# Moving one VectorE pass over the second weight ahead of the turns of batch 1's query features

## The chip, the cores and the metric

The kernel runs on one core of a Trainium2 chip. The metric is the device time of one execution in microseconds (us); before the change the median of three runs is 103.25 us. Engines are named as in the profile: PE is TensorE (matmuls), DVE is VectorE, ACT is ScalarE, POOL is GpSimd, SP is SyncE, which here only issues DMAs.

## What is computed

A linear attention with sketched features, and behind it a block with a hidden layer and a residual:

```python
# q, k, v: (4, 4, 1088, 32) f32; S1, S2: (8, 32)
def phi(x):
    a = np.einsum('rd,bhsd->bhsr', S1, x)
    b = np.einsum('rd,bhsd->bhsr', S2, x)
    return np.einsum('bhsi,bhsj->bhsij', a, b).reshape(*x.shape[:-1], r * r)
q_p, k_p = (phi(q), phi(k))
kv = np.einsum('bhsf,bhsd->bhfd', k_p, v)
z = np.sum(k_p, axis=2)
num = np.einsum('bhsf,bhfd->bhsd', q_p, kv)
den = np.einsum('bhsf,bhf->bhs', q_p, z)[..., None] + 1e-06
x = (num / den)      # heads side by side: (4, 1088, 128)
...
xn = (x - mu) / np.sqrt(var + 1e-06) * g_ln
ch = np.maximum(xn @ w_ch1, 0.0) @ w_ch2      # (128, 512), (512, 128)
return (x + ch).astype(np.float32)
```

The sketches and the two weights come as 64-bit floats. The chip's engines compute in 32 bits here, so the kernel builds 32-bit floats out of the two words of each number.

## The kernel before

All steps of the four batches are small functions ("ops"), and one long string, `PROGRAM` (line 910), lists their calls in the order in which they are issued. An op's instructions go to the engine that its function or its first argument names (V is VectorE, A ScalarE, G GpSimd, S SyncE's DMA queue), and each engine works through its own instructions in the order of the list. Between engines only data and buffers make one wait for another. So a call's place in the list matters against the other calls of its own engine.

The second weight (`w2` in the code, words numbered 2) goes through these passes, all on 128 x 512 words:

- `w_bits` (line 281): VectorE cuts the fraction bits out of each high word, one `tensor_scalar` with a bitwise and.
- `w_mant` (line 294): ScalarE makes the mantissa of them.
- `w_ex` (line 276): VectorE cuts the exponent out of the high words; ScalarE's `w_exf` and `w_e2` work on it, and VectorE's `w_e3` joins it with the sign.
- `w_add` and `w_mul`: GpSimd adds the low word's part to the mantissa, and multiplies.

Around the change, batch 0's rows enter the hidden layer, batch 1's query features are made, and batch 2's keys are begun. There are eight PSUM banks, A, B, C, D, M, N, O and K. The ops in question:

- `turn_g k 2` and `turn_r k 2` (lines 432 and 448): VectorE transposes the key rows of batch 2 into `kT`.
- `q_feat 1` (line 625): TensorE makes batch 1's query features, head h into bank A, B, C or D.
- `q_tok 1 h` (line 637): VectorE turns head h's features out of its bank into `fq`, here called the turn of bank B, A, D or C (heads 1, 0, 3, 2 in this order). It sets the bank free.
- `hid z c j` (line 841): TensorE multiplies batch 0's rows with block j of the first weight into bank z; `relu` (line 847) takes it out on ScalarE. The order of the banks is O, N, M, K, B, D, C; the last three need a turn to be over.
- `q_turn 4 9` (line 676): VectorE transposes a part of batch 0's query products, `qp`.
- `k_feat 2` (line 503): TensorE makes batch 2's key features in banks A and B, and `k_tok 2` (line 515) turns them on VectorE.
- `k_prod G 1 0 5`, `sk_qq 3` and `k_prod G 1 5 9` (lines 521 and 424): GpSimd forms the key products of batch 1 in two parts, with a small copy between them. All of its operands lie in SBUF.
- `k_val 1` (line 558): TensorE multiplies these products with batch 1's values, in bank K.

SyncE's queue holds, at the same place in the list, the loads of keys and queries of batches 2 and 3 (`ld`, line 111) and of the values.

Of the kernel before, what the change touches and what calls it, by code (L numbers as in the profile page):

```python
# [24 lines left out]
def kernel(  # L25
# [21 lines left out]
    B, H, S, D = q.shape  # L47
# [4 lines left out]
    G = S // 32  # L52
# [15 lines left out]
    M, KV = [banks["M"]], banks["K"]  # L68
# [863 lines left out]
    q_flip 2 4 0 C; ld_v S 1 2; q_flcp A 2 4 1 A; k_zs 1; f_spr B; q_flip 0 2 0 O; turn_h q 1 1;  # L932
    q_flcp A 2 4 0 C; ld_v S 1 1; f_rcp A B; q_flip 0 2 1 D; q_flcp A 0 2 0 O; k_sc 1;
    turn_h q 1 0; ld_vr S 1 1; num0 2 4 N; q_flcp A 0 2 1 D; k_sccp V 1; num0 0 2 O; turn_r k 2;
    k_prod G 1 0 5; num0_cp A 2 4 N; turn_g k 2 0 4; kv_rd S 0; q_feat 1 0 9; num0_cp A 0 2 O;
    ld_v S 1 0; hid O 0 0 0 2; q_tok 1 1 0 9; ld_vr S 2 0; hid N 0 2 2 4; q_tok 1 0 0 9;
    relu A O 0 0 0 2; ld S k 3 0 34; hid M 0 2 0 2; w_bits V 2 0 512; sk_qq 3; ld S q 2 0 34;
    hid K 0 3 0 2; k_prod G 1 5 9; q_tok 1 3 0 9; ld S q 3 0 34; hid B 0 1 2 4; q_tok 1 2 0 9;
    hid D 0 0 2 4; q_turn 4 9; relu A B 0 1 2 4; hid C 0 1 0 2; w_mant A 2 0 512; k_feat 2 0 9;
    relu A K 0 3 0 2; q_ac G 1 4 9; relu A C 0 1 0 2; relu A M 0 2 0 2; q_ac G 1 0 4; k_val 1;  # L940
# [96 lines left out]
```

## Time and profile before

| what | before |
| --- | --- |
| time, median of 3 runs (lowest to highest) | 103.25 us (103.06 to 103.25) |
| the profiled execution: time | 103.13 us |
| the profiled execution: span of the core | 101.3 us |
| granted TensorE clock, mean | 1.0 |
| TensorE busy | 95.2 us, 94% |
| VectorE busy | 71.5 us, 71% |
| ScalarE busy | 40.6 us, 40% |
| GpSimd busy | 60.5 us, 60% |

The span is the time from the first to the last instruction of the profiled execution; its time is longer by what lies before and behind. Busy shares are means over the whole span. A timeline row gives the start in us from the start of the span, the duration, the engine, the line, the operation, and "out<-in" with partitions x elements; in square brackets stands how long the engine sat idle before it, and what ended that. A line like L82 is that of a helper that several ops use. The starts of instructions that follow each other on an engine often lie a little before the end of the one in front.

### The profile page before, as it was taken

What the parts mean: (1) busy time and instruction counts of PE and PEld (TensorE: products, weight loads), DVE (VectorE), ACT (ScalarE), POOL (GpSimd) and SP (SyncE); (2) the same over time, 40 slices, a digit from 0 to 9 for tenths busy, and PEclk for the clock granted to TensorE, in tenths of its full rate; (3) what the DMA queues carried; (4) which work ended last, traced back from release to release, by engine and by line L of the source; (5) the groups of instructions that cost most, each with busy time, mean ns of one, the idle gap of its engine ahead of it and who ended that gap; (6) DMA issues with size and microseconds to landing.
All of it is one profiled execution on the core that took longest, in us unless ns stands there. A gap on an engine that the chain in (4) does not pass through costs nothing.

```text
span 101.3 us, 3442 instructions
## 1 busy us (share of the span) xinstructions
PE 95.2 (94%) x1348; PEld 68.8 (68%) x1348; DVE 71.5 (71%) x234; ACT 40.6 (40%) x118; POOL 60.5 (60%) x84
## 2 busy tenths in 40 slices
PE   5989999997999999999999999999999999999970
PEld 4856865855574597874686896864388985489950
DVE  1598999779998896989517889567239848483540
ACT  4465517653764900054482405456861004040300
POOL 7137979997377999300299997999529230004700
PEclk9999999999999999999999999999999999999999
DMA  2899991047954166623052720257244744630441
GB/s 86 283 315 399 354 323 44 10 128 193 380 204 123 56 193 206 181 60 129 6 179 73 177 46 6 83 173 209 85 117 102 223 151 134 183 108 0 104 109 46
DMA packets 14863, 15.16 MB, mean 150 GB/s; under 512 B 4096, under 2 KB 11136, under 8 KB 14848
## 3 DMA queue, kind: packets, MB, share of 16 engines
q1 hardware_dynamic: 13680, 13.61, 43.0%
q10 hardware_dynamic: 1168, 1.35, 5.3%
q8 instruction: 10, 0.16, 0.6%
q14 instruction: 5, 0.04, 0.1%
HBM read 10.42 MB, written 4.52 MB: 148 GB/s over the span
## 4 chain that ended last, share of the span: by engine, by line
PE 85%; DVE 6%; DMA 2%; ACT 1%; issue 1%; SPq 0%; DVEq 0%
PE bankO L859 8%; PE bankK L859 6%; PE bankN L859 6%; PE bankM L859 5%; PE bankD L843 5%; PE bankA L843 5%; PE bankK L561 5%; PE bankN L843 4%; PE bankM L250 4%; PE bankB L843 4%; PE bankM L843 4%; PE bankC L843 3%; PE bankA L735 3%; PE bankA L507 3%; PE bankC L859 3%; PE bankO L843 3%
## 5 line engine op out<-in xcount | busy, mean ns | idle before, releaser
L827 POOL TENSOR_SCALAR va<-mv 128x4 f32<-128x4 f32 (+1 forms) x10 | 2.3, 227 | 24.4 <-DVE mv L822 15.5
L82 POOL TENSOR_TENSOR kp<-kf 128x1280 f32<-128x1280 f32 (+4 forms) x9 | 15.7, 1749 | 1.9 <-PE bankK L561 1.8
L82 POOL TENSOR_TENSOR qp<-a,fq 128x1280 f32<-128x1280 f32 (+1 forms) x7 | 15.4, 2205 | 0.3
L677 DVE STREAM_TRANSPOSE qpT<-qp 128x1280 f32<-128x1280 f32 (+1 forms) x7 | 9.7, 1385 | 3.8 <-POOL qp L82 3.7
L250 PE MATMUL bankM<-ones 128*128 128x256 f32 (+1 forms) x34 | 9.3, 415 | 1.2 <-DVE top L180 1.2
L829 POOL TENSOR_TENSOR rstd<-va,mhalf 128x4 f32<-128x4 f32 (+1 forms) x10 | 9.4, 943 | 0.8
L859 PEld LDWEIGHTS bankO<-w,hT 128*128 128x128 f32 x64 | 7.6, 192 | 1.4 <-issue 0.9
L250 PEld LDWEIGHTS bankM<-ones 128*128 128x128 f32 x34 | 6.8, 223 | 2.6 <-DVE top L180 1.2
L859 PE MATMUL bankO<-w,hT 128*128 128x128 f32 x64 | 8.4, 280 | 0.0
L859 PEld LDWEIGHTS bankN<-w,hT 128*128 128x128 f32 x56 | 6.9, 192 | 1.4 <-issue 1.0
L859 PEld LDWEIGHTS bankK<-w,hT 128*128 128x128 f32 x56 | 6.9, 192 | 1.4 <-issue 1.4
L859 PE MATMUL bankK<-w,hT 128*128 128x128 f32 x56 | 7.3, 277 | 0.0
L816 DVE BATCH_NORM_STATS2 st<-x 128x6 f32<-128x128 f32 x32 | 6.8, 276 | 0.5 <-DMA x<-xd 0.5
L859 PE MATMUL bankN<-w,hT 128*128 128x128 f32 x56 | 7.1, 275 | 0.0
L797 DVE STREAM_TRANSPOSE xh<-xT 128x512 f32<-128x512 f32 x8 | 5.5, 690 | 2.1 <-ACT xT L77 2.0
L843 PE MATMUL bankD<-xT,w 128*128 128x512 f32 (+1 forms) x12 | 5.8, 566 | 0.8 <-DVE fq L639 0.8
L851 ACT ACTIVATE hT<-bankD 128x512 f32<-128x512 f32 (+1 forms) x6 | 3.4, 564 | 7.8 <-DMA x<-xd 7.3
L859 PEld LDWEIGHTS bankM<-w,hT 128*128 128x128 f32 x48 | 5.8, 192 | 0.9 <-issue 0.9
L859 PE MATMUL bankM<-w,hT 128*128 128x128 f32 x48 | 6.1, 277 | 0.0
L735 PE MATMUL bankD<-qpT,kvr 32*32 32x288 f32 (+1 forms) x64 | 5.9, 386 | 0.0
L735 PE MATMUL bankC<-qpT,kvr 32*32 32x288 f32 (+1 forms) x64 | 5.9, 386 | 0.0
L735 PE MATMUL bankB<-qpT,kvr 32*32 32x288 f32 (+1 forms) x64 | 5.8, 386 | 0.0
(227 smaller groups left out, 249.3 us busy)
## 6 DMA issues: line engine op xcount, KB each, us to landing
xd<-xh SPq DMA_DIRECT2D x8, 256.0 KB, 2.0
x<-xd SPq DMA_DIRECT2D x32, 64.0 KB, 2.0
kn<-in_k_dram SPq DMA_DIRECT2D x3, 544.0 KB
qn<-in_q_dram SPq DMA_DIRECT2D x3, 544.0 KB, 7.0
vn<-in_v_dram SPq DMA_DIRECT2D x12, 128.0 KB, 2.6
out_dram<-ob ACTq DMA_DIRECT2D x19, 64.0 KB, 1.9
out_dram<-ob SPq DMA_DIRECT2D x13, 64.0 KB, 3.6
w_raw<-in_moe_w_ch_dram SPq DMA_DIRECT2D x2, 256.0 KB, 5.0
```

Source lines behind the costliest of these rows:

```text
L82: by[eng].tensor_tensor(out=o, in0=a, in1=b, op=ALU.mult)
L250: pe.matmul(M[0][:, 0:w], ones[:, 0:P], ones[:, 0:w], start=True, stop=True)
L507: pe.matmul(X[hp][32 * g : 32 * g + 32, 32 * u0 : 32 * u0 + w], sk8[64 * hp : 64 * hp + 64, :], _ap(kT[b % 2], 64 * hp, 64, 32 * g + P * u ...
L561: pe.matmul(KV[D * h : D * h + D, 0:F], vn[b][:, TW * h + D * u : TW * h + D * (u + 1)], kp[:, H * F * u + F * h : H * F * u + F * (h + 1) ...
L677: dve.transpose(_ap(qpT, 0, P, 32 * u0, [[32, u1 - u0], [TW, 8], [1, 32]]), qp[:, H * F * u0 : H * F * u1])
L735: pe.matmul(X[r][D * h : D * h + D, o : o + w], kvr[b % 2][rows, F * h + D * f : F * h + D * f + D], qpT[rows, c : c + w], start=(f == 0), ...
L797: dve.transpose(_ap(xh[slot(c)], 0, P, 0, [[32, n], [32 * n, 4], [1, 32]]), cols(c))
L816: dve.bn_stats(out=sts[slot(c)][:, 6 * t : 6 * t + 6], in_=row_ap(c, t))
L829: pool.tensor_tensor(out=rstds[slot(c)][:, 0:n], in0=vas[slot(c)][:, 0:n], in1=mhalf[:, 0:n], op=ALU.pow)
L843: pe.matmul(banks[z][:, 0:n], w1[:, P * j : P * (j + 1)], cols(c)[:, a : a + n], start=True, stop=True)
L851: act.activation(o, i, AF.Relu)
L859: pe.matmul(banks[z][:, DM * t : DM * (t + 1)], h[:, 512 * j + P * t : 512 * j + P * (t + 1)], w2[:, DM * j : DM * (j + 1)], start=(j == 0 ...
```

## The change

The call `w_bits V 2 0 512` moves up in the list, from behind `hid M 0 2 0 2` to behind `turn_g k 2 0 4`. In VectorE's own order it stood between the turns of banks A and D, and now stands ahead of all four, behind the key transposes of batch 2. The calls that it passes in the list and that aren't VectorE's keep their order on their engines.

```diff
-    k_prod G 1 0 5; num0_cp A 2 4 N; turn_g k 2 0 4; kv_rd S 0; q_feat 1 0 9; num0_cp A 0 2 O;
-    ld_v S 1 0; hid O 0 0 0 2; q_tok 1 1 0 9; ld_vr S 2 0; hid N 0 2 2 4; q_tok 1 0 0 9;
-    relu A O 0 0 0 2; ld S k 3 0 34; hid M 0 2 0 2; w_bits V 2 0 512; sk_qq 3; ld S q 2 0 34;
+    k_prod G 1 0 5; num0_cp A 2 4 N; turn_g k 2 0 4; w_bits V 2 0 512; kv_rd S 0; q_feat 1 0 9;
+    num0_cp A 0 2 O; ld_v S 1 0; hid O 0 0 0 2; q_tok 1 1 0 9; ld_vr S 2 0; hid N 0 2 2 4;
+    q_tok 1 0 0 9; relu A O 0 0 0 2; ld S k 3 0 34; hid M 0 2 0 2; sk_qq 3; ld S q 2 0 34;
     hid K 0 3 0 2; k_prod G 1 5 9; q_tok 1 3 0 9; ld S q 3 0 34; hid B 0 1 2 4; q_tok 1 2 0 9;
```

## The prediction, made before the change was run

> **What bounds the kernel now.** I read the page first, then the waits of TensorE, then the chain of work that ended last, and last the timelines of the four engines around the edit.
>
> ```profile
> span 101.3 us, 3442 instructions
> ```
>
> ```profile
> PE bankM L250 <- DVE top L180: 1.2, 1, 1.2
> PE bankD L843 <- DVE fq L639: 0.8, 1, 0.8
> PE bankA L507 <- DVE kT L452: 0.5, 1, 0.5
> PE bankK L561 <- ACT vn L77: 0.2, 1, 0.2
> ```
>
> These four rows are all that TensorE ever waits for (columns: total us, times, longest). Apart from the first, which is the start of the program, the largest is one wait of 0.8 us: a hidden-layer matmul into bank D, held up by VectorE's turn of batch 1's query features (fq, line 639). A span that is TensorE work from end to end gets shorter only where such a wait goes. The chain shows what is in front of this one:
>
> ```profile
> 23.43 1.66 DVE bits L282
> 25.09 0.40 DVE fq L639
> ```
>
> The chain leaves TensorE for the first pass over the second weight's words, `w_bits` (line 282), 1.66 us of it, and comes back through the turn of head 3. So the moved instruction itself is on the path. VectorE's timeline around it (start, duration):
>
> ```profile
> 20.77 1.21 DVE L434 STREAM_TRANSPOSE kT<-kn 128x1024 f32<-128x1024 f32 x1
> 22.59 0.48 DVE L639 STREAM_TRANSPOSE fq<-bankB 128x288 f32<-128x288 f32 x1 [0.61 <-PE bankD L629]
> 22.99 0.44 DVE L639 STREAM_TRANSPOSE fq<-bankA 128x288 f32<-128x288 f32 x1
> 23.36 1.73 DVE L282 TENSOR_SCALAR bits<-w_raw 128x512 uint32<-128x512 uint32 x1
> 25.01 0.47 DVE L639 STREAM_TRANSPOSE fq<-bankD 128x288 f32<-128x288 f32 x1
> 25.41 0.43 DVE L639 STREAM_TRANSPOSE fq<-bankC 128x288 f32<-128x288 f32 x1
> 25.77 1.46 DVE L677 STREAM_TRANSPOSE qpT<-qp 128x1280 f32<-128x1280 f32 x1
> 27.49 0.48 DVE L517 STREAM_TRANSPOSE kf<-bankB 128x288 f32<-128x288 f32 x1 [0.25 <-PE bankB L507]
> 28.26 0.39 DVE L277 TENSOR_SCALAR ex<-w_raw 128x512 uint32<-128x512 uint32 x1
> ```
>
> `w_bits` takes 1.73 us. The last row is the same kind of instruction, with the same shape and the same input (`w_ex`), and takes 0.39. So some 1.34 us of `w_bits` is a stall, and it isn't a semaphore, because the instruction counts as running. GpSimd's timeline shows what runs beside it:
>
> ```profile
> 20.39 2.38 POOL L82 TENSOR_TENSOR kp<-kf 128x1280 f32<-128x1280 f32 x1
> 22.71 0.19 POOL L425 COPY skq<-skq 128x16 f32<-128x16 f32 x1
> 22.86 1.94 POOL L82 TENSOR_TENSOR kp<-kf 128x1024 f32<-128x1024 f32 x1
> 25.93 0.94 POOL L82 TENSOR_TENSOR ac<-fq 128x160 f32<-128x160 f32 x2 [1.12 <-DVE fq L639]
> 28.62 1.95 POOL L82 TENSOR_TENSOR kp<-kf 128x1024 f32<-128x1024 f32 x1 [1.76 <-PE bankK L561]
> ```
>
> The product of the key features (third row) ends at 22.86 + 1.94 = 24.80, and `w_bits` ends at 23.36 + 1.73 = 25.09, 0.29 later, a little less than its own 0.39. It reads as if `w_bits` stood until GpSimd's instruction was over and then ran. `w_ex` had the same work and met no GpSimd instruction: nothing ran there until 28.62. An early place shows the same between the two engines, in the first fence VectorE, in the second GpSimd:
>
> ```profile
> 4.05 0.16 DVE L207 TENSOR_TENSOR m<-bit,head 128x4 f32<-128x4 int32 x1
> 5.01 0.44 DVE L207 TENSOR_TENSOR m<-bit,head 128x2 f32<-128x2 int32 x1
> ```
>
> ```profile
> 4.98 0.45 POOL L82 TENSOR_TENSOR s_f<-mant,bits 16x128 f32<-16x128 f32 x1 [2.27 <-DVE bit L206]
> ```
>
> The mask of half the size takes 0.44 instead of 0.16 us and ends (5.45) just behind the GpSimd product that began before it (5.43).
>
> The Trainium skill, "SBUF — State Buffer", section "Who interferes with whom", has a rule for this that speaks against the new place as well: VectorE and GpSimd share a pair of ports, a `tensor_scalar` may need it, and whoever begins first keeps it for a whole instruction while the other stands. The trace agrees at 24.80 and 5.43. By that rule `w_bits` stands at the new place too, behind the product that began at 20.39; were there no such rule, it would take 0.39 there, and the sum below would come out the same, as the turns it delays have time to spare.
>
> **The change part by part.** One VectorE instruction moves. It issues no DMA; what it passes on its own engine are the turns of banks B and A (heads 1 and 0). The loads, matmuls and activations between the two places in the listing are on other engines, whose own order stays. Nothing is added or removed.
>
> *Its new place.* The key transpose in front ends at 20.77 + 1.21 = 21.98; VectorE then sat idle for 0.61 us, until TensorE gave it the query features at 22.59. `w_bits` begins at about 21.9, in the middle of GpSimd's product of 20.39, which ends at 22.77. I take it that VectorE gets its turn there: it ends at 22.77 + 0.29 = 23.06. No row shows `w_bits` at a place like this. Bounds: 22.3, if nothing holds it up (21.9 + 0.39), and 25.09, if it also stands through the two GpSimd instructions behind (second and third row of that fence). I take 23.06, since both rows with a stall end just behind the GpSimd instruction that had begun before, and one row, if a weak one, has such a change of turns, VectorE first and GpSimd second:
>
> ```profile
> 14.62 0.25 DVE L355 TENSOR_SCALAR cg<-ident,g_raw 128x128 f32<-128x128 f32 x1
> ```
>
> ```profile
> 13.99 0.72 POOL L323 TENSOR_TENSOR mant<-mant,low 128x256 f32<-128x256 f32 x1
> 14.78 0.53 POOL L82 TENSOR_TENSOR ac<-fq 128x160 f32<-128x160 f32 x1
> ```
>
> This `tensor_scalar` began beside one GpSimd instruction (over at 14.71), ended at 14.87, and the next one, begun at 14.78, took 0.53 where the pair of 25.93 took 0.47 each. So VectorE got in between. But GpSimd had a gap of 0.07 there, while at 22.7 its rows overlap.
>
> *The turns.* With starts 0.40, 0.37 and 0.36 apart as in the rows: B at 23.0 (0.4 later than now), A at 23.4, D at 23.77 to 24.24, C at 24.13 to 24.56. D ends 1.24 earlier than now (25.48), C 1.28 earlier (25.84).
>
> *TensorE behind them.*
>
> ```profile
> 23.66 0.59 PE L843 MATMUL bankK<-xT,w 128*128 128x256 f32 x2
> 24.09 0.59 PE L843 MATMUL bankB<-xT,w 128*128 128x256 f32 x2
> 25.54 0.70 PE L843 MATMUL bankD<-xT,w 128*128 128x256 f32 x2 [0.85 <-DVE fq L639]
> 26.07 0.59 PE L843 MATMUL bankC<-xT,w 128*128 128x256 f32 x2
> 26.60 0.43 PE L507 MATMUL bankA<-kT,sk 64*32 64x288 f32 x1
> 27.24 1.21 PE L561 MATMUL bankK<-kp,vn 128*32 128x64 f32 x72
> ```
>
> Bank B is needed at 24.09 and is turned at 23.48: 0.6 to spare, so the 0.4 costs nothing. The matmuls before B follow each other every 0.43 (23.66 to 24.09). Bank D's then begins at 24.52 (its turn is over 0.28 before) and bank C's at 24.95 (0.39 before). C's was at 26.07: **1.12 us** go, 0.85 of them the wait and the rest the slow start behind it (0.70, and 0.53 to the next). Then the key features follow at 25.48 and the key-value product at 26.12.
>
> *What is late next.* ScalarE:
>
> ```profile
> 24.72 0.39 ACT L851 ACTIVATE hT<-bankB 128x256 f32<-128x256 f32 x1 [1.34 <-PE bankB L843]
> 25.12 0.72 ACT L296 ACTIVATE mant<-bits,one 128x512 f32<-128x512 uint32 x1
> 25.75 0.36 ACT L851 ACTIVATE hT<-bankK 128x256 f32<-128x256 f32 x1
> ```
>
> Key features need bank B emptied: 25.11, against 25.48. The key-value product needs bank K emptied: 26.11, or about 26.0, as `mant` no longer waits for the bits; against 26.12. That one is close and may take back up to 0.05. It also needs GpSimd's second product, which begins some 0.25 later and ends at about 25.1: in time. VectorE's long turn of qp runs from 24.5 to 25.95, before bank B's keys (25.48 + 0.89 = 26.37). `w_ex` then comes at about 27.1 and is over at 27.5, when GpSimd's next product begins (28.62 − 1.1): no new stall, but by some hundredths only.
>
> *Loads don't come earlier.* The key rows of batch 3 are the first such input behind the edit; the queue's row, then DMA by the microsecond (last two columns: share of the engines, GB/s):
>
> ```profile
> 23.10 0.43 SPq L113 DMA_DIRECT2D kn<-in_k_dram  x1
> ```
>
> ```profile
> 28.00:29.00 1.00, 1.00 (x76) 0.79 (x70) 1.00 (x4) 0.32 (x1) 0.38 (x1) 1.00 0.94 383
> 29.00:30.00 1.00, 1.00 (x51) 0.71 (x48) 0.85 (x5) 0.78 (x4) 1.00 (x1) 1.00 0.24 77
> ```
>
> They are the first of three large loads issued one after another, and all three are through at about 29.0, so the first, by its third of the bytes, lands at about 26.5; VectorE will want it at 28.7, as its part there follows the key features. From there on what the four engines do hangs on work that itself moves up, GpSimd's product of the second weight too:
>
> ```profile
> 32.49 1.28 POOL L82 TENSOR_TENSOR w<-mant,bits 128x512 f32<-128x512 f32 x1 [0.69 <-DVE bits L318]
> ```
>
> It waits for VectorE's last pass over the words, which by the code waits for ScalarE's passes and these for `w_ex`.
>
> **Sum:** 1.12, less up to 0.05 at bank K: 1.05 to 1.12. The profiled execution took 103.13 us (its span of 101.3 and 1.8 around it), so 102.0 to 102.1; the median of the runs, 103.25, lies 0.12 higher. I say **102.1**.
>
> **The rivals.**
>
> *GpSimd keeps its turn (slower).* Place: 22.77. Its three instructions overlap in the trace (22.71 before 22.77, 22.86 before 22.90); if VectorE gets in only where GpSimd really pauses, `w_bits` ends at 25.09 as now, but now with all four turns behind it: B at 25.01, A 25.41, D 25.78, C 26.14 to 26.57. TensorE stands from 24.09 on; bank B's matmul begins at 25.54, C's at 26.63 instead of 26.07, and the rest 0.56 later: **103.7**. It decides against the change as soon as `w_bits` ends later than some 24.3: bank D's turn ends 1.18 behind it (24.24 − 23.06) and the matmul begins 0.06 after that (25.54 − 25.48), which is 25.54 as now. For it: the overlap. Against: an instruction that waits already should be served at the first release.
>
> *Given back downstream.* 1.1 us come off TensorE at 26, but a step with little to spare (bank K, `w_ex` meeting GpSimd's product, a later turn or load) stops some of it. If `w_ex` came behind the start of that product, it would stand up to 1.95 us, and the second weight with it. For it: TensorE waits nowhere else now, so room behind isn't shown by waits. Against: the steps I followed all move with TensorE. **102.4 to 102.9**.
>
> *Nothing.* The order isn't what sets it, for instance if `w_bits` ends near 24.3: **103.1**.
>
> **How the numbers follow.** Forecast 0.64, given back 0.14, nothing 0.04, GpSimd keeps its turn 0.18. About 0.2% (0.2 us) is what a measurement of this kernel can tell from no change. Faster: 0.64 + 0.14 = 0.78; same 0.04; slower 0.18. The range from 101.8 (the full sum and 0.2 for runs) to 103.3 holds the first three cases, 0.82; the forecast's own is 101.9 to 102.3.
>
> **What would show it.** `w_bits` begins at 21.9 and ends near 23.06, GpSimd's copy or second product starts or ends some 0.25 later, the wait at bank D is gone from TensorE's waits, bank C's matmul is at about 24.95 and the key-value product at 26.1 to 26.2. Wrong if `w_bits` ends at 25.1 (then bank B's matmul carries the wait), or if TensorE's waits after 26 show a new row.

## The result, and the profile after

| what | before | after |
| --- | --- | --- |
| time, median of 6 runs each (lowest to highest) | 103.15 us (102.96 to 103.25) | 102.12 us (102.09 to 102.56) |
| ratio to before, 95% interval | | 0.9909 (0.9890 to 0.9928) |
| the profiled execution: time | 103.13 us | 102.09 us |
| the profiled execution: span | 101.3 us | 100.3 us |

The kernel is 0.9% faster, 1.03 us by the medians. Forecast were 102.1 us and a range of 101.8 to 103.3.

TensorE's waits of the changed kernel (total us, times, longest):

```profile
PE bankM L250 <- DVE top L180: 1.2, 1, 1.2
PE bankK L561 <- ACT vn L77: 0.2, 1, 0.2
```

The wait at bank D is gone. So is the 0.5 us for the first keys, which lies ahead of the edit. Nothing was won by that: in this execution TensorE's first 14 matmuls (line 250, the start of the program) took 5.48 us instead of 4.37, so TensorE came to the first key features at 7.50 instead of 6.91, and the keys were there. VectorE's timeline:

```profile
20.89 1.20 DVE L434 STREAM_TRANSPOSE kT<-kn 128x1024 f32<-128x1024 f32 x1
22.02 1.15 DVE L282 TENSOR_SCALAR bits<-w_raw 128x512 uint32<-128x512 uint32 x1
23.08 0.47 DVE L639 STREAM_TRANSPOSE fq<-bankB 128x288 f32<-128x288 f32 x1
23.48 0.43 DVE L639 STREAM_TRANSPOSE fq<-bankA 128x288 f32<-128x288 f32 x1
23.84 0.43 DVE L639 STREAM_TRANSPOSE fq<-bankD 128x288 f32<-128x288 f32 x1
24.21 0.43 DVE L639 STREAM_TRANSPOSE fq<-bankC 128x288 f32<-128x288 f32 x1
```

and GpSimd's:

```profile
20.49 2.38 POOL L82 TENSOR_TENSOR kp<-kf 128x1280 f32<-128x1280 f32 x1
22.82 0.39 POOL L425 COPY skq<-skq 128x16 f32<-128x16 f32 x1
23.17 1.94 POOL L82 TENSOR_TENSOR kp<-kf 128x1024 f32<-128x1024 f32 x1
```

Read the two together. `w_bits` still takes 1.15 us where 0.39 would do: it stands until GpSimd's product ends (20.49 + 2.38 = 22.87) and is over 0.30 later (23.17). The second row shows the other side of the same thing: now GpSimd's copy stands. It takes 0.39 us instead of the 0.19 of before, and the product behind it begins as `w_bits` ends. What has changed is when `w_bits` stands: in the 0.6 us in which VectorE had nothing to do, and not for the whole of the second product.

TensorE:

```profile
24.21 0.59 PE L843 MATMUL bankB<-xT,w 128*128 128x256 f32 x2
24.64 0.59 PE L843 MATMUL bankD<-xT,w 128*128 128x256 f32 x2
25.07 0.59 PE L843 MATMUL bankC<-xT,w 128*128 128x256 f32 x2
26.24 1.21 PE L561 MATMUL bankK<-kp,vn 128*32 128x64 f32 x72
```

Bank D's matmul follows bank B's after 0.43. Bank B's is 0.12 later than in the profile of before (24.09). That much this execution had lost at its start: the matmuls that come right behind the first key features begin at 8.15 instead of 8.03. Bank C's is 1.00 earlier (26.07 before). From bank B to bank C it is 0.86 instead of 1.98: the 1.12 us of the sum. The key-value product is 1.00 earlier as well (27.24 before), and so is VectorE's last instruction, here after and then before:

```profile
96.72 0.35 DVE L872 SCALAR_TENSOR_TENSOR ob<-bankK,rstd,xr 128x128 f32<-128x128 f32 x1 [0.60 <-PE bankK L859]
```

```profile
97.72 0.35 DVE L872 SCALAR_TENSOR_TENSOR ob<-bankK,rstd,xr 128x128 f32<-128x128 f32 x1 [0.60 <-PE bankK L859]
```

Nothing that was won at 25 us was given back in the 70 us behind it.

### The profile page after: what moved, and what is told of

Read it like the earlier page. It is cut to its first block, busy times and chain, and to the rows that moved or that the text cites. A ratio compares the mean times of both kernels' runs of the same rounds, so it can differ in the third digit from the quotient of the medians.

```text
span 100.3 us, 3442 instructions
## 1 busy us (share of the span) xinstructions
PE 95.6 (95%) x1348; PEld 69.5 (69%) x1348; DVE 70.8 (71%) x234; ACT 40.4 (40%) x118; POOL 60.7 (61%) x84
## 4 chain that ended last, share of the span: by engine, by line
PE 93%; ACT 1%; DVE 1%; issue 0%; DVEq 0%
PE bankM L250 9%; PE bankO L859 8%; PE bankK L859 6%; PE bankN L859 6%; PE bankM L859 6%; PE bankD L843 5%; PE bankA L843 5%; PE bankN L843 5%; PE bankK L561 5%; PE bankB L843 4%; PE bankM L843 4%; PE bankC L843 3%; PE bankA L735 3%; PE bankC L859 3%; PE bankO L843 3%; PE bankA L507 2%
## 5 line engine op out<-in xcount | busy, mean ns | idle before, releaser
L250 PE MATMUL bankM<-ones 128*128 128x256 f32 (+1 forms) x34 | 10.4, 457 | 1.2 <-DVE top L180 1.2
L250 PEld LDWEIGHTS bankM<-ones 128*128 128x128 f32 x34 | 7.5, 249 | 2.8 <-DVE top L180 1.2
L735 PE MATMUL bankA<-qpT,kvr 32*32 32x288 f32 (+1 forms) x64 | 5.8, 384 | 0.0
```

What stands on the lines that cost most here:

```text
L250: pe.matmul(M[0][:, 0:w], ones[:, 0:P], ones[:, 0:w], start=True, stop=True)
L735: pe.matmul(X[r][D * h : D * h + D, o : o + w], kvr[b % 2][rows, F * h + D * f : F * h + D * f + D], qpT[rows, c : c + w], start=(f == 0), ...
```

## The experiments

The theory is that `w_bits` stands while a GpSimd instruction that began before it runs, that it is served when that one ends, and that the time is set by whether bank D's and C's turns are over when TensorE comes to them. The rivals are that `w_bits` is slow for another reason, that earlier is simply better, and that GpSimd keeps its turn. Ratios are to the kernel before, timed beside each group (medians 103.24 us for experiments 1 to 4, 103.23 for 5 to 8).

**1. Without GpSimd's second product, the order of before.**

```diff
-    hid K 0 3 0 2; k_prod G 1 5 9; q_tok 1 3 0 9; ...
+    hid K 0 3 0 2; q_tok 1 3 0 9; ...
```

> The order of before, but GpSimd's second product of batch 1's keys is left out (the values are then multiplied with old products; the work beside it is missing on purpose). Theory of the lock: the pass over the words at its old place meets no GpSimd instruction, takes 0.38 to 0.40 us instead of 1.73, bank D's matmul doesn't wait (about 24.5 instead of 25.54), and the time is 102.0 to 102.2. Rival, that the pass is slow of itself at this place (the loads that run beside it, its strided input): it still takes some 1.7 us, TensorE's wait of 0.8 us stays, and the time is about 103.1. Rival of order, that only what stands in front of the turns counts: some gain smaller than 1 us with the wait left in part.

Measured: 102.21 us (4 runs, 101.92 to 102.41), ratio 0.9904 (0.9872 to 0.9937). VectorE, with `w_bits` at its old place, between the turns of A and D:

```profile
23.10 0.44 DVE L639 STREAM_TRANSPOSE fq<-bankA 128x288 f32<-128x288 f32 x1
23.46 0.39 DVE L282 TENSOR_SCALAR bits<-w_raw 128x512 uint32<-128x512 uint32 x1
23.77 0.47 DVE L639 STREAM_TRANSPOSE fq<-bankD 128x288 f32<-128x288 f32 x1
```

The pass takes 0.39 us, and bank D's matmul doesn't wait:

```profile
24.63 0.59 PE L843 MATMUL bankD<-xT,w 128*128 128x256 f32 x2
```

So what stretched the pass to 1.73 was GpSimd's product, and its place cost something through that alone: at the old place the ratio is now about that of the change (0.9909). The strided input is the same, and loads ran beside the pass here as well (226 GB/s from 23.46 to 23.85), so it was neither of them.

**2. One place up instead of to the front.**

```diff
-    ... hid N 0 2 2 4; q_tok 1 0 0 9;
-    relu A O 0 0 0 2; ld S k 3 0 34; hid M 0 2 0 2; w_bits V 2 0 512; ...
+    ... hid N 0 2 2 4; w_bits V 2 0 512; q_tok 1 0 0 9;
+    relu A O 0 0 0 2; ld S k 3 0 34; hid M 0 2 0 2; ...
```

> The pass moves up by one turn only, between the turns of banks B and A. Theory of the lock: it begins at about 23.0, just behind the start of GpSimd's second product, and stands until that ends at 24.8; it takes 2.1 us and ends at 25.1 as before, now with three turns behind it instead of two, so bank D's matmul comes at about 25.9 instead of 25.54 and the time is 103.5, slower than before by 0.3 to 0.4. Rival, that earlier is better step by step: between 102.3 and 103.0.

Measured: 103.65 us (10 runs, 103.48 to 103.83), ratio 1.0040 (1.0024 to 1.0057): slower than before. VectorE, then GpSimd, then TensorE's wait:

```profile
23.15 2.10 DVE L282 TENSOR_SCALAR bits<-w_raw 128x512 uint32<-128x512 uint32 x1
25.18 0.47 DVE L639 STREAM_TRANSPOSE fq<-bankA 128x288 f32<-128x288 f32 x1
```

```profile
23.03 1.93 POOL L82 TENSOR_TENSOR kp<-kf 128x1024 f32<-128x1024 f32 x1
```

```profile
PE bankD L843 <- DVE fq L639: 1.2, 1, 1.2
```

The pass begins 0.12 behind the start of the second product, so it stands through all of it (23.03 + 1.93 = 24.96, the pass ends at 25.25). Begun earlier, it ends no earlier, and now three turns wait behind it instead of two. Bank D's wait grows from 0.8 to 1.2 us. "Earlier is better" is refuted.

**3. Behind all four turns.**

```diff
-    ... hid M 0 2 0 2; w_bits V 2 0 512; sk_qq 3; ...
+    ... hid M 0 2 0 2; sk_qq 3; ...
-    hid D 0 0 2 4; q_turn 4 9; ...
+    hid D 0 0 2 4; w_bits V 2 0 512; q_turn 4 9; ...
```

> The pass moves down instead, behind all four turns and ahead of the turn of the query products. Theory: the turns run at 22.6, 23.0, 23.36 and 23.73 and TensorE doesn't wait for them; the pass begins at about 24.1, stands until 24.8, ends at 25.1 (1.0 us); the long turn then ends at 26.5, about when batch 2's keys are there. Time 102.0 to 102.3, as with the change. Rival, that the pass has to come earlier than before to gain anything (its reader on ScalarE, the mantissa, held up): 103.0 or more.

Measured: 102.16 us (10 runs, 101.89 to 103.36), ratio 0.9910 (0.9879 to 0.9942), the same gain as with the change, by a move the other way. TensorE's two waits are those of the changed kernel. VectorE:

```profile
23.59 0.44 DVE L639 STREAM_TRANSPOSE fq<-bankC 128x288 f32<-128x288 f32 x1
23.95 1.01 DVE L282 TENSOR_SCALAR bits<-w_raw 128x512 uint32<-128x512 uint32 x1
24.88 1.50 DVE L677 STREAM_TRANSPOSE qpT<-qp 128x1280 f32<-128x1280 f32 x1
```

The pass stands 0.6 us here too, but what waits behind it is the long turn of `qp`, which has time. So the pass was needed hardly any earlier or later; it had only to be out of the way of bank D's and C's turns. One small price shows in the rows alone. The key-value product begins 1.27 us behind bank C's matmul (24.82, 26.09) instead of 1.17 as in the changed kernel. It reads as the step at bank K that the prediction called close: ScalarE's `mant` begins only at 24.99, with the pass over at 24.96, and the `relu` behind it empties bank K at 25.98, which is 1.16 behind bank C's matmul instead of 1.03. The medians can't tell 0.1 us.

**4. GpSimd's two long products one right behind the other** (from the changed kernel).

```diff
-    ... hid M 0 2 0 2; sk_qq 3; ld S q 2 0 34;
-    hid K 0 3 0 2; k_prod G 1 5 9; q_tok 1 3 0 9; ...
+    ... hid M 0 2 0 2; ld S q 2 0 34;
+    hid K 0 3 0 2; k_prod G 1 5 9; sk_qq 3; q_tok 1 3 0 9; ...
```

> The changed kernel with GpSimd's small copy moved behind its second product, so that the two long products follow each other directly. Theory, that the waiting VectorE instruction is served when the running GpSimd instruction ends: the pass still ends at about 23.1, the second product now takes some 0.25 longer, time 102.0 to 102.2. Rival of the prediction, that GpSimd keeps its turn where its instructions follow without a pause and that the small copy let VectorE in: the pass ends at about 24.9 and the time is 103.5 to 103.8.

Measured: 102.58 us (10 runs, 101.69 to 102.93), ratio 0.9928 (0.9900 to 0.9956). VectorE, then GpSimd's products (both in one row: 20.61 to 25.09), then what TensorE waits for near the edit:

```profile
22.13 1.17 DVE L282 TENSOR_SCALAR bits<-w_raw 128x512 uint32<-128x512 uint32 x1
23.22 0.47 DVE L639 STREAM_TRANSPOSE fq<-bankB 128x288 f32<-128x288 f32 x1
```

```profile
20.61 4.48 POOL L82 TENSOR_TENSOR kp<-kf 128x1280 f32<-128x1280 f32 x2
```

```profile
PE bankK L561 <- DMA vn<-in_v_dram: 0.4, 1, 0.4
```

The pass ends at 23.30, 0.29 behind the end of the first product (20.61 + 2.40 = 23.01), though GpSimd made no pause there. The rival "GpSimd keeps its turn" is refuted for an instruction of VectorE that already waits, and the small copy isn't what let it in. The time lies between the two expectations, though. In the profiled execution (102.67 us) most of the difference is the last row, which no earlier profile had: the key-value product, which TensorE now reaches earlier, waits 0.4 us for batch 1's values. Whether the other nine executions waited too, and whether this order on GpSimd has a part in it, no run shows.

**5. The pass twice** (from the changed kernel).

```diff
-    turn_g k 2 0 4; w_bits V 2 0 512; ...
+    turn_g k 2 0 4; w_bits V 2 0 512; w_bits V 2 0 512; ...
```

> The changed kernel with the pass issued twice in a row at its new place (the second writes the same words again). It asks what room the new place has. Theory: the first ends at about 23.1; GpSimd's small copy, which waited, has the ports next; the second pass stands behind the copy only (some 0.2 us) and ends at about 23.5. By the starts in the profiles bank D's matmul is held up once the pass ends later than about 23.3 (its turn ends 1.2 behind the pass, the matmul comes at 24.5 to 24.6), so TensorE waits some 0.2 to 0.3 us there and the time is 102.3 to 102.5. Rival, that the second pass finds GpSimd's second product before it: it ends at 25.1 to 25.4, all four turns come behind it, and the time is 103.7 to 104.1.

Measured: 104.12 us (10 runs, 103.97 to 104.31), ratio 1.0077 (1.0058 to 1.0097). The theory's time was missed; it came out as the rival's, 0.02 above its range. VectorE (both passes in one row), then GpSimd, then the line's durations (shortest, median, longest):

```profile
22.03 3.40 DVE L282 TENSOR_SCALAR bits<-w_raw 128x512 uint32<-128x512 uint32 x2
25.34 0.47 DVE L639 STREAM_TRANSPOSE fq<-bankB 128x288 f32<-128x288 f32 x1
```

```profile
22.85 0.40 POOL L425 COPY skq<-skq 128x16 f32<-128x16 f32 x1
23.20 1.94 POOL L82 TENSOR_TENSOR kp<-kf 128x1024 f32<-128x1024 f32 x1
```

```profile
L282 DVE TENSOR_SCALAR bits<-w_raw x2: 1166/1681/2196, 22.0 to 23.2; 128x512 uint32<-128x512 uint32 x2
```

The second pass takes 2.20 us and ends at 25.43, so it began at 23.23, by 0.03 behind the second product. It ends 0.29 behind that product's end (25.14), as in experiment 2. I had let it begin while the copy ran. By the rows the copy's own time overlaps this start (22.85 + 0.40 = 23.25), but the product had already begun. Every turn is behind the pass now, and TensorE waits at bank B:

```profile
PE bankB L843 <- DVE fq L639: 1.5, 1, 1.5
```

It is the prediction's slow rival, brought about by a pass that comes too late by the start of one instruction. In all these runs the rows agree that what counts is which of the two began first.

**6 to 8. The values' load earlier; with the pass behind the turns; the change again.** In 6 and 7 the load stands ahead of the read of the key-value product, for which SyncE's queue has to wait:

```diff
-    ... w_bits V 2 0 512; kv_rd S 0; q_feat 1 0 9; num0_cp A 0 2 O; ld_v S 1 0; hid O 0 0 0 2; ...
+    ... w_bits V 2 0 512; ld_v S 1 0; kv_rd S 0; q_feat 1 0 9; num0_cp A 0 2 O; hid O 0 0 0 2; ...
```

Kernel 7 has this and experiment 3's place of the pass; kernel 8 is the changed kernel itself.

> The changed kernel with one load of batch 1's values issued ahead of the read of the key-value product on SyncE's queue, some 0.6 to 0.9 us earlier. In the profile of the run with the copy behind, TensorE waited 0.4 us for these values. Theory, that with the change this load has become the next limit in some executions: no wait for the values in the profile, the lowest times as with the change (101.7 to 102.1), the highest ones lower, the median 102.0 to 102.1. Rival, that the spread comes from elsewhere (the first loads): median and spread as with the change, or the read of the key-value product, now later by 0.2 to 0.5 us, costs something.

> The pass behind all four turns, as in the run of that place, and the values' load earlier. Theory: TensorE waits for nothing between 22 and 96, as in each part alone; time 101.9 to 102.1, the changed kernel's or a little under it by the values' load alone, as there is no wait left that the place of the pass could take away. Rival, that the turns being earlier by 0.5 us is worth something of its own: under 101.8.

> The changed kernel itself again, beside the others on the same chip. Both theories expect 102.0 to 102.3; it is there to show its spread, and whether it waits for the values in this profile.

| kernel | median (lowest to highest, 6 runs each) | ratio to before (95% interval) |
| --- | --- | --- |
| 6, values earlier | 102.02 us (101.96 to 102.39) | 0.9873 (0.9845 to 0.9901) |
| 7, behind the turns, values earlier | 102.22 us (102.05 to 102.41) | 0.9887 (0.9859 to 0.9914) |
| 8, the change again | 102.32 us (101.93 to 103.09) | 0.9898 (0.9861 to 0.9935) |

The change again gains what it gained. None of the three shows a wait for the values in its profile, kernel 8 without the earlier load included, so these profiles don't test the earlier load. Kernel 6 has the lowest median and kernel 7 lies above its forecast of 101.9 to 102.1, but the intervals of 6, 7 and 8 overlap: whether the earlier load is worth anything stays open. The profiles of 6 to 8 also have a wait ahead of the edit, for the first key features, in 6 and 7 and then in 8:

```profile
PE bankA L507 <- ACT exf L310: 0.4, 1, 0.4
```

```profile
PE bankA L507 <- DVE kT L452: 0.7, 1, 0.7
```

Such a wait isn't a loss by itself: kernels 6 and 7 come to bank B's matmul at 24.16 and 24.08, the changed kernel's own profile without the wait at 24.21. Kernel 8 comes to it at 24.41, 0.20 later, and its profiled execution is 0.24 us longer (102.33 against 102.09), so there most of the difference lies ahead of the edit. Where the spread of the other runs comes from isn't shown.

## Why the prediction was right, point by point

- *The stall.* Right: 1.34 of the 1.73 us were GpSimd's second product (experiment 1: 0.39 us without it). The sentence further up that between engines only data and buffers make one wait for another is too narrow, then: here one engine stood for another with neither between them.
- *The new place.* Right in duration and mechanism: 1.15 us, forecast 21.9 to 23.06; in this execution, in which everything near the edit lies 0.1 later, 22.02 to 23.17. The choice between the bounds 22.3 and 25.09, which rested on two rows with a stall and one weak row with a change of turns, holds for a pass that waits already (experiment 4). It doesn't hold for one that begins just behind the second product (experiments 2 and 5). The time alone wouldn't show this step: bank D's turn is over at 24.27 and its matmul begins at 24.64, so a pass without any stall, or one that ended some 0.3 us later, would have given the same time.
- *The turns and TensorE.* Bank D's turn 1.24 earlier, forecast; measured, it ends at 24.27 instead of 25.48, which is 1.21, and 1.33 with the 0.12 taken off. Bank C's matmul came 0.43 behind D's, as forecast, and the slow start after the wait went with it: 1.12.
- *What is late next.* Bank K was free in time (emptied at 25.73 + 0.37 = 26.10, needed at 26.24), so the "up to 0.05" wasn't needed. With the pass behind the turns it was (experiment 3). The second product began 0.31 later (0.19 with the offset taken off), and nobody waited for it. `w_ex` met no product: in the profile after, it ends 0.02 us behind the start of the next one, as close as feared, and still takes 0.38.
- *Loads.* The step that was wrong, though the total didn't suffer: I named the keys of batch 3 as the first load behind the edit. The first one is batch 1's values, read by the key-value product at 26.24, and in one profile (experiment 4) they were 0.4 us late.
- *The sum.* 1.05 to 1.12 forecast, 1.04 us between the two profiled executions and 1.03 between the medians. It is 1.12 at the edit, and this profiled execution came there 0.12 later than the one of before.
- *The rivals.* "GpSimd keeps its turn" gives a slower kernel under another condition than I gave. Not whether GpSimd pauses decides, but whether VectorE's instruction has begun before GpSimd's next one. Its price, 0.56 us over before, was 0.9 in experiment 5. Two things were missing from it: bank D's matmul, held up as well, takes 0.53 to the next one, so that by the prediction's own rows bank C's comes at 26.80 and not at 26.63; and the pass ended at 25.43 instead of 25.09, of which 0.13 is that execution's later start. That gives 0.56 + 0.17 + 0.21 = 0.94, against 0.89 by the medians.
- *The rule.* A start 0.12 us behind that of GpSimd's product made the pass 1.71 us longer (2.10 instead of 0.39, experiment 2), and one 0.03 us behind 1.81 (2.20, experiment 5). The Trainium skill ("SBUF — State Buffer", section "Who interferes with whom") has the rule that whoever begins first keeps the shared ports for the whole instruction. The runs agree in the standing, by the durations just given; that it is ports which the two engines share, no run here shows.

## What to carry to other kernels

An instruction that takes several times as long as its like, with no wait in front of it, may be standing: look on the neighbouring engine for an instruction whose end lies just before its own. Then move it so that it begins while a short rest of that instruction is left, or so that what is queued behind it has time; an earlier place is worth nothing if it falls just behind the neighbour's next start. When such a wait goes, list what the bottleneck engine reads next, its loads too.

## What was not expected of the hardware

- VectorE got in between two GpSimd products without a pause between them (experiment 4), for which only one weak row spoke beforehand. The pass ended at 23.30, and the second product, on record while VectorE still waited, took 2.14 us instead of 1.94:

```profile
L82 POOL TENSOR_TENSOR kp<-kf x2: 2136/2268/2399, 20.6 to 23.0; 128x1280 f32<-128x1280 f32 x1, 128x1024 f32<-128x1024 f32 x1
```

- The margin is small: of two equal passes, the one that began 0.03 us behind a GpSimd product stood until that was over (experiment 5). Rows that follow each other on an engine overlap (the copy ends at 23.25, the product behind it begins at 23.20), so the exact margin isn't known; that the pass stood through the product is, by its 2.20 us.
- Not every VectorE instruction stands. In the changed kernel the turns of banks A, D and C (0.43 us each, from 23.48 on) run wholly beside GpSimd's second product (23.17 to 25.11), and without that product, in experiment 1, they take 0.44 to 0.47.
